# A list-scheduled attention and mixture kernel on one core: the planner's weights and its assumed DMA landing time replaced

## The chip, the core and the metric

One core of a Trainium2 chip runs the whole program. The metric is device microseconds of one execution; several executions of a kernel are timed and their median is given. TensorE is called PE here (its weight loads PEld), VectorE DVE, ScalarE ACT, GpSimd POOL, and SP is the engine whose queue issues all the DMAs. L12 is line 12 of the kernel. The changed kernel has one line more in its table and two more in `build`, so a line of the changed kernel stands 3 higher than the same line before; the text uses the numbers of the kernel before.

## What is computed

```python
# attention: batch 4, heads 8, sequence 576, head size 64, causal, with a bias from a cumulative sum
cum = np.cumsum(np.maximum(s, 0.0), axis=-1)
bias = -(cum[:, :, :, None] - cum[:, :, None, :])
scores = np.where(causal, -1000000000.0, scale * q @ k.T + np.minimum(bias, 0.0))
x = softmax(scores) @ v                      # 2304 tokens x 512
# first layer
h = x @ w_in                                 # 512 x 1024
solu = h * softmax(h)
x = (layernorm(solu) * g_ln) @ w_out         # 1024 x 512
# second layer
h = maximum(maximum(x @ w1, x @ w2), x @ w3) # 512 x 768 each
out = h @ w_out2                             # 768 x 512
```

## The kernel before

All inputs are float32. The kernel computes every matrix product from float16 halves: a value is split into a high half and a low half (the rest), and three products (high high, high low, low high) are added in PSUM. Much of the work outside PE is this splitting. Weights come in as float32 words and are unpacked once (`load_w`): L608, L612 and L615 on DVE sort the bits of a piece of 512 columns into a PSUM accumulator, L620 on ACT writes the high half, L622 on DVE the low half. There are 40 such pieces.

The 2304 tokens are 18 tiles of 128: four blocks of 128 rows for each of two sequences (`c` = 0, 1), then one tail tile with the last 64 rows of both, and the same again for the other two sequences. Score widths are 128, 256, 384 and 512 columns for the blocks and 576 for the tail. For each tile `prep` loads k, q and v and splits them (`st`, `vs`), `scores` makes the score matmuls of a pair of heads (L788, L794), a maximum on DVE (L825, L858) and the exponential on ACT (L877, into `r`), and splits the probabilities into `es`; the last 64 columns of a tail tile go into `est`. A DMA transposes `es` into `et` and `est` into `ett` (L904, L911). `values` multiplies by v (L961, for tails L942 and L948) and normalises into `f` (L995). `m1` is the first layer's first product (L1034) with its softmax and layer norm (L1048 to L1096) into `ln` and, transposed, `lnt`. Each two tiles make a group, for which follow `m2` (L1131), the three products of `m3` with their running maximum (L1170, L1189), and `m4` (L1204), whose rows go out. The first four tiles are transposed on PE instead (L474, L488), with ACT or DVE copying the halves out of PSUM (L481, L484, L491, L492).

`split_ops` makes the two steps of a split. Each can stand on several engines: the high half (L405 on ACT, L407 on DVE or POOL), the low half on DVE as one instruction (L434) or on POOL as two, a scaling in place (L441) and a subtraction (L444). L1095 (DVE or POOL) or L1096 (ACT) scales `e`.

The order of all this is not written by hand. `Schedule.run` replays the program in a model: each operation has a duration for each engine it may stand on, a position `pos` (its urgency, a tile number shifted by the weights in the table `P`: `la`, `wi`, `w3`, `o2` and so on) and its dependences and buffers. The engine that can begin something first takes the operation with the smallest `pos` among those that could begin then. Where an operation may stand on several engines, `spare` is added to the end on each (DVE, ACT, POOL; first three numbers up to position `spare_until`, the next three after), and the smallest sum decides. A DMA is taken to land `LAT_DMA` (ns) after its share of the queue's traffic. The model holds POOL and those DVE operations that are not in `ALONE` apart: one runs at a time. The order that the replay gives is what is emitted, engine by engine; on the chip each engine runs its list in order.

```python
    LAT_SAME, LAT_CROSS, LAT_DMA, LAT_ISSUE = 130, 180, 1250, 650
...
                    end = t + o.alts[c[1]][1] + sp[e] - 1
...
                o.end = dma + self.LAT_DMA
```

Of the kernel before, what the change touches and what calls it, by code (L numbers as in the profile page):

```python
# [30 lines left out]
MINUS_ONES = -(1.0 + 0xBF80 * 2.0 ** -23)  # L31

P = dict(
    la=8.4,
    lp=-1.469,
    lu=-13.333,
    lv=-0.647,
    o1=-3.616,
    o2=-4.09,
    o3=-0.398,  # L40
    o4=0.334,
    ds=1.887,
    wi=-20.819,
    wid=2.708,
    wo=-15.551,
    wod=-18.167,
    w3=6.958,
    w3d=1.141,
    w4=-16.623,
    w4d=15.675,  # L50
    mp=-1.93,
    look=[2.7, 0.0, 35.7, 169.7, 69.9],
    spare=[1764.9, 1665.2, 1871.5, 968.8, -1500.0, 3960.7, 27.5],
    n_st=4,
    gs=[2, 2, 2, 2, 2, 2, 2, 2, 2],
    wa=["ldq0", "ldq0", "c00", "c00"],
    nf=3,
    net=4,
    nr=3,
    lc=-23.89,  # L60
    S=[],
    ep=[0],
    pt=[4, 4, 4, 4],
# [288 lines left out]
def build(nc, T, X, dims):  # L352
# [15 lines left out]
    size = [len(ts) * 128 for ts in groups]  # L368
    due = [ts[-1] for ts in groups]
    S_ = Schedule(P["look"], P["spare"], P["off"], P["eng"])  # L370

    def unit(name, tile=""):
        S_.unit, S_.tile = name, tile

    op = S_.op
    pools = {}
# [126 lines left out]
    def scaled(k):  # L503
        return k in P["S"] or f"{k}@{S_.tile}" in P["S"]

# [646 lines left out]
    def m3(g, f0):  # L1152
# [11 lines left out]
        for w in range(3):  # L1164
            ps, first = buf("acc"), ([], [])
            for f in (f0, f0 + 1):
                for kk in range(KD):
# [8 lines left out]
                    o.after.update(before)  # L1176
                    S_.hold(o, m)
                    o.after.update(first[f % 2])
# [68 lines left out]
    for k, n in enumerate(P["wa"]):  # L1247
        if n in named:
            for i in range(2):
                if ("w", k, i) in named:  # L1250
                    named["w", k, i].after.add(named[n])
    return S_, pools


@with_exitstack
def fox_attention_solu_max3_kernel(
# [71 lines left out]

    X = dict(q=q, k=k, v=v, s=s, w_in=w_in, w_out=w_out, g_ln=g_ln, w1=w1, w2=w2, w3=w3, w_out2=w_out2, out=out)
    sched, pools = build(nc, T, X, (B, H, S, D, DFF, DF2))  # L1330
    sched.run()
    with tc.manual_schedule():
# [34 lines left out]
```

## Time and profile before

| | us |
|---|---|
| median of 3 runs | 676.64 (675.38 to 676.77) |
| the profiled execution | 676.31, span 674.6 |
| PE busy | 621.2 (92%) |
| DVE busy | 464.3 (69%) |
| ACT busy | 301.8 (45%) |
| POOL busy | 34.1 (5%) |

An engine's busy time is the union of its instructions; PE's weight loads run beside its matmuls. Windows are in us from the start of the span. In the rows below, "[1.29 <-DMA ett<-est]" is the time that the engine was idle before the row, and what ended it.

### The profile page before, as it was taken

Reading aid. Unit: us, or ns where it says so; the run is one execution under the profiler, and the core shown is the slowest. Engines: PE = TensorE matmul, PEld = TensorE weight load, DVE = VectorE, ACT = ScalarE, POOL = GpSimd, SP = SyncE. Lnnn points to the kernel's source line nnn. Section 1 sums busy time; section 2 is a strip of 40 time slices with the busy share of each in tenths; the row PEclk is TensorE's granted clock in tenths of the full one; section 3 lists DMA queues with packets and bytes.
Section 4 is the critical chain, followed back from the end, with each engine's and each line's share of the span. In section 5 each row is a group of like instructions: output and inputs, shape, how many; then the busy total and the mean of one; then the engine's idle time right before and its main releaser. Section 6 shows DMA issues by size and latency. Waiting matters only on the chain.

```text
span 674.6 us, 15275 instructions
## 1 busy us (share of the span) xinstructions
PE 621.2 (92%) x6188; PEld 442.7 (66%) x6188; DVE 464.3 (69%) x1109; ACT 301.8 (45%) x713; POOL 34.1 (5%) x49
## 2 busy tenths in 40 slices
PE   1579888899999999899999999989999999999997
PEld 1334556777576666667666675659767867878774
DVE  7899999997799678798888988775155245212121
ACT  3678875554476445667556546351023022110110
POOL 1101000010001101020000201000000000000000
PEclk9998999999999999999999999989999999999999
DMA  6976755569989879699999896864032022000001
GB/s 176 276 216 176 171 153 162 172 144 186 170 167 176 155 142 150 131 186 189 162 181 174 152 181 119 127 99 84 1 63 63 1 48 48 1 32 2 17 17 32
DMA packets 249351, 82.68 MB, mean 123 GB/s; under 512 B 225472, under 2 KB 244096, under 8 KB 249280
## 3 DMA queue, kind: packets, MB, share of 16 engines
q1 hardware_dynamic: 249280, 81.70, 60.0%
q8 instruction: 48, 0.79, 0.5%
q14 instruction: 23, 0.19, 0.1%
HBM read 35.95 MB, written 4.83 MB: 60 GB/s over the span
## 4 chain that ended last, share of the span: by engine, by line
PE 63%; DVE 15%; DMA 14%; issue 3%; ACT 3%; SPq 1%; POOL 0%; DVEq 0%; POOLq 0%; ACTq 0%
PE acc L1170 23%; PE acc L1131 11%; PE acc L1204 9%; PE h L1034 8%; DMA et<-es 7%; PE sc L794 4%; PE av L961 3%; PE sc L788 2%; DVE acc L612 2%; DVE acc L615 2%; DVE r L825 1%; DMA kt<-in_moe_w_in_dram 1%; DMA vs<-in_moe_w_in_dram 1%; DVE f L608 1%; DMA lnt<-ln 1%
## 5 line engine op out<-in xcount | busy, mean ns | idle before, releaser
L1170 PE MATMUL acc<-x2A,w_h 128*128 128x256 f16 x1296 | 215.5, 273 | 2.3 <-DVE f L1189 1.5
L1170 PEld LDWEIGHTS <-w_h 128*128 128x128 f16 x1944 | 187.3, 98 | 32.6 <-issue 7.6
L1170 PE MATMUL acc<-x2B,w_h 128*128 128x256 f16 x648 | 176.7, 273 | 0.0
L877 ACT ACTIVATE r<-r,mn 128x128 f32<-128x128 f32 (+4 forms) x144 | 83.0, 578 | 55.0 <-DVE mn L825 39.7
L1034 PE MATMUL h<-w_in_h,xt 128*128 128x512 f16 x432 | 101.3, 380 | 0.0
L1131 PE MATMUL acc<-lnt,w_out_h 128*128 128x256 f16 x864 | 98.2, 273 | 1.1 <-DMA lnt<-ln 1.0
L1131 PEld LDWEIGHTS <-w_out_h 128*128 128x128 f16 x864 | 83.4, 98 | 13.3 <-issue 3.3
L1189 DVE TENSOR_TENSOR f<-f,acc 128x512 f32<-128x512 f32 x54 | 36.9, 684 | 69.8 <-PE acc L1170 69.8
L1034 PEld LDWEIGHTS <-xt 128*128 128x128 f16 x432 | 40.0, 98 | 45.7 <-issue 3.6
L454 ACT ACTIVATE f<-acc 128x512 f32<-128x512 f32 x37 | 22.0, 595 | 98.5 <-PE acc L1170 57.9
L1204 PE MATMUL acc<-w2o_h,h2A 128*128 128x512 f16 x216 | 64.4, 380 | 0.0
L825 DVE CUSTOM_DVE_ANT_0 r<-sc,mask 128x128 f32<-128x128 f32 (+3 forms) x128 | 58.7, 485 | 7.1 <-PE sc L794 5.5
L434 DVE SCALAR_TENSOR_TENSOR es<-r,es 128x512 f16<-128x512 f32 (+1 forms) x89 | 56.7, 642 | 2.3 <-ACT es L405 1.7
L794 PE MATMUL sc<-kt,qt 64*128 64x256 f16 (+2 forms) x768 | 47.9, 264 | 0.7 <-DMA kt<-st 0.4
L961 PE MATMUL av<-vs,et 128*128 128x64 f16 x960 | 38.1, 195 | 5.1 <-DMA et<-es 4.8
L961 PEld LDWEIGHTS <-et 128*128 128x128 f16 x960 | 34.9, 99 | 12.0 <-DMA et<-es 7.7
L405 ACT ACTIVATE es<-r 128x512 f16<-128x512 f32 (+1 forms) x48 | 28.0, 584 | 29.4 <-DMA et<-es 25.5
L1204 PE MATMUL acc<-w2o_h,h2B 128*128 128x512 f16 x108 | 41.0, 379 | 0.0
L1055 ACT ACTIVATE ln<-e,st 128x1024 f32<-128x1024 f32 x18 | 20.7, 1150 | 42.4 <-DVE e L1048 35.7
L788 PE MATMUL sc<-ckr,cqr 6*128 6x128 bf16 (+5 forms) x192 | 28.6, 308 | 11.9 <-DMA cqr<-cum_d 9.8
L794 PEld LDWEIGHTS <-qt 64*128 64x128 f16 (+1 forms) x864 | 26.8, 99 | 18.3 <-issue 11.2
L454 ACT ACTIVATE x2A<-acc 128x512 f16<-128x512 f32 x16 | 9.5, 593 | 64.0 <-PE acc L1131 64.0
(138 smaller groups left out, 721.3 us busy)
## 6 DMA issues: line engine op xcount, KB each, us to landing
kt<-in_moe_w_dram SPq DMA_DIRECT2D x18, 256.0 KB
vs<-in_moe_w_dram SPq DMA_DIRECT2D x18, 256.0 KB
raw<-in_k_dram SPq DMA_DIRECT2D x16, 256.0 KB
raw<-in_q_dram SPq DMA_DIRECT2D x16, 256.0 KB
raw<-in_v_dram SPq DMA_DIRECT2D x16, 256.0 KB
out_dram<-f SPq DMA_DIRECT2D x16, 256.0 KB
kt<-in_moe_w_out_dram SPq DMA_DIRECT2D x7, 512.0 KB
vs<-in_moe_w_out_dram SPq DMA_DIRECT2D x7, 512.0 KB
```

The costliest lines, as they stand in the source:

```text
L434: nc.vector.scalar_tensor_tensor(out=lo(g), in0=src(g), scalar=sc1(g), in1=hi(g), op0=ALU.mult, op1=ALU.subtract)
L454: nc.scalar.activation(out=out(*a), in_=in_(*a), func=AF.Copy, scale=scale)
L788: yield lambda: nc.tensor.matmul(out=out(), lhsT=T["cqr"][cr, hp, cs], rhs=T["ckr"][cr, hp, ck], start=True, stop=False, skip_group_check= ...
L794: yield lambda n=n, qa=qa, o=o, kx=kx: nc.tensor.matmul(out=out()[:, o], lhsT=qv()[r, qa * HP + hp, ts], rhs=kx, start=False, stop=(n == 2 ...
L825: nc.vector.tensor_tensor_reduce(out=gw(R)[:, g], in0=gw(sc[y])[:, g], in1=T["mask"][:, SM - W:SM], scale=1.0 / S_MUL, scalar=3e38, op0=AL ...
L877: nc.scalar.activation(out=gw()[:, g], in_=gw()[:, g], func=AF.Exp, bias=mnf()[:, g:g + 1], scale=-1.0, accum_out=den(hs[g]),)
L961: nc.tensor.matmul(out=out, lhsT=ea_[:, ea, kb], rhs=T["v_s"][c, kb // 2][:, kb % 2, ha + a, va], start=(kb == 0 and m == 0), stop=(kb == ...
L1034: nc.tensor.matmul(out=hb()[:, n * 512:(n + 1) * 512], lhsT=xt()[:, xa, kk], rhs=T["w_in_h"][:, wa, kk, n * 512:(n + 1) * 512], start=(kk ...
L1131: nc.tensor.matmul(out=ps()[:, d % 2 * GN:(d % 2 + 1) * GN], lhsT=T["w_out_h"][:, wa, kk, d * 128:(d + 1) * 128], rhs=lnt()[:, la, kk], st ...
L1170: nc.tensor.matmul(out=ps()[:, f % 2 * GN:(f % 2 + 1) * GN], lhsT=T["w123_h"][:, w, wa, f, kk], rhs=x2(xa)[:, kk], start=(kk == 0 and i == ...
L1189: op([("DVE", dve2(2 * GN), lambda ps=ps: nc.vector.tensor_tensor(out=m(), in0=m(), in1=ps(), op=ALU.max))], pk + [m], [m], pos, kind="m3x")
L1204: nc.tensor.matmul(out=ps(), lhsT=h2(ha)[:, f, o * 128:(o + 1) * 128], rhs=T["w2o_h"][:, wa, f], start=(f == 0 and i == 0), stop=(f == KF2 ...
```

## The change

The numbers of the table `P` are replaced, and the model's landing time becomes a number of the table, 1.7 us where 1.25 stood. No instruction's shape and no arithmetic is changed; order and choice of engine come out of the same replay.

```diff
 P = dict(
-    la=8.4,
+    la=7.686,
...
-    w3=6.958,
-    w3d=1.141,
+    w3=11.379,
+    w3d=2.467,
...
-    look=[2.7, 0.0, 35.7, 169.7, 69.9],
-    spare=[1764.9, 1665.2, 1871.5, 968.8, -1500.0, 3960.7, 27.5],
+    look=[0.0, 0.0, 35.7, 25.4, 16.3],
+    spare=[1756.4, 1670.1, 1222.0, 2565.6, -1500.0, 5079.4, 23.5],
...
-    lc=-23.89,
+    lat=1.7,
+    lc=-29.521,
...
     S_ = Schedule(P["look"], P["spare"], P["off"], P["eng"])
 
+    S_.LAT_DMA = int(P["lat"] * 1000)
+
```

What the new order holds, by count over the whole program: the instructions of PE are the same in number and kind. Of the high halves (L405, L407), 104 stood on ACT, 91 on DVE and 16 on POOL; now 70 stand on ACT, none on DVE and 141 on POOL. Of the low halves, 12 stood on POOL (L444), now 48, and DVE's L434 fall from 199 to 163. L1095 falls from 10 to 0 on DVE and rises from 0 to 12 on POOL.

The first place is POOL's list where the first L1204 matmul comes (`vs`, `st` and `es` are halves of v, of k and q, and of the probabilities; `raw` is what was loaded). Before:

```order
L407 TENSOR_SCALAR st_87<-raw_85 128x512
L407 TENSOR_SCALAR h2A_112<-f_114 128x512
L441 TENSOR_SCALAR raw_85<-raw_85 128x512
L444 TENSOR_TENSOR st_86<-raw_85,st_86 128x512
L441 TENSOR_SCALAR r_90<-r_90 128x384
```

The last row stands behind the first L1204 matmul. After the change:

```order
L410 TENSOR_SCALAR st_87<-raw_84 128x512
L444 TENSOR_SCALAR raw_84<-raw_84 128x512
L447 TENSOR_TENSOR st_87<-raw_84,st_87 128x512
L1098 TENSOR_SCALAR e_106<-e_106,st_123 128x1024
...
L1098 TENSOR_SCALAR e_106<-e_106,st_124 128x1024
L410 TENSOR_SCALAR h2A_112<-f_116 128x512
L410 TENSOR_SCALAR st_86<-raw_84 128x512
L410 TENSOR_SCALAR vs_73<-raw_85 128x8x64
...
L410 TENSOR_SCALAR es_93<-r_90 128x384
L410 TENSOR_SCALAR es_93<-r_92 128x384
L410 TENSOR_SCALAR es_94<-r_90 128x384
```

Three more rows of `es`, with two of `vs` and `st` among others, follow ahead of the first L1204 matmul. POOL now makes halves of k, q, v and of the probabilities, and scales `e`: up to there it had ten such instructions and now has 33.

The second place is PE near the end of the attention, between the last score matmuls of the last head pair of the last tile and the value matmuls of the head pair ahead of it, which read `ett` and `et`. Before:

```order
L794 MATMUL sc_126<-k_tail,qt_89 64x64
L1204 LDWEIGHTS h2A_112
L1204 MATMUL acc_131<-w2o_h,h2A_112 128x512
...
L1170 LDWEIGHTS w_h
L1170 MATMUL acc_129<-x2A_110,w_h 128x256
...
L942 LDWEIGHTS ett_101
L942 MATMUL av_127<-v_tail,ett_101 128x64
```

Between them stand 12 matmuls of 512 columns (L1204) and 6 of 256 (L1170). After the change:

```order
L797 MATMUL sc_126<-k_tail,qt_89 64x64
L1207 LDWEIGHTS h2A_112
L1207 MATMUL acc_131<-w2o_h,h2A_112 128x512
...
L1207 MATMUL acc_129<-w2o_h,h2A_112 128x512
...
L945 LDWEIGHTS ett_101
L945 MATMUL av_127<-v_tail,ett_101 128x64
```

Now 15 matmuls of 512 columns stand there. Over the whole way from the scores of that head pair to its value matmuls, it is 21 of 512 and 6 of 256 before, and 30 of 512 after.

The third place is PE behind its first score matmuls (`r` are the first probabilities, `acc` the three accumulators that weights are unpacked in as well). Before:

```order
L794 MATMUL sc_126<-kt_68,qt_88 128x128
L474 MATMUL acc_131<-k_tail,r_90 128x128 x4
L474 MATMUL acc_129<-k_tail,r_91 128x128 x4
L488 LDWEIGHTS k_tail
L488 MATMUL acc_131<-et_97,k_tail 128x512
```

After the change:

```order
L797 MATMUL sc_126<-kt_68,qt_88 128x128
L477 MATMUL acc_130<-k_tail,r_90 128x128 x4
L477 MATMUL acc_131<-k_tail,raw_85 128x128 x4
L491 LDWEIGHTS k_tail
L491 MATMUL acc_130<-et_97,k_tail 128x512
```

The first probabilities are transposed into another accumulator, and a tile of k comes ahead of the second ones.

## Rows read from the trace of the kernel before

**Rows 1.** The page, first part: busy time, share of the span, instructions.

```profile
PE 621.2 (92%) x6188; PEld 442.7 (66%) x6188; DVE 464.3 (69%) x1109; ACT 301.8 (45%) x713; POOL 34.1 (5%) x49
```

**Rows 2.** Three stretches: length, each engine's busy time (instructions), granted clock, DMA share, GB/s.

```profile
0.00:131.60 131.60, 95.70 (x768) 61.87 (x769) 122.19 (x289) 85.44 (x201) 9.03 (x19) 0.99 0.69 189
131.60:450.00 318.40, 305.55 (x3573) 211.37 (x3573) 266.25 (x679) 178.49 (x433) 24.81 (x29) 1.00 0.90 158
450.00:674.60 224.60, 219.98 (x1852) 169.46 (x1849) 75.84 (x143) 37.84 (x80) 0.24 (x1) 0.99 0.14 33
```

**Rows 3.** PE's waits: what ended them, us in total, times, longest.

```profile
PE sc L788 <- DMA cqr<-cum_d: 9.8, 2, 8.8
...
PE av L961 <- DMA et<-es: 4.8, 9, 1.0
PE av L942 <- DMA ett<-est: 3.3, 2, 2.0
...
PE acc L1131 <- DMA lnt<-ln: 1.0, 1, 1.0
```

**Rows 4.** PE in order of time, four rows behind idle time: start, us.

```profile
17.04 0.55 PE L788 MATMUL sc<-ckr,cqr 6*128 6x128 bf16 x2 [8.85 <-DMA cqr<-cum_d]
...
25.69 1.94 PE L474 MATMUL acc<-k_tail,r 128*128 128x128 f32 x8 [5.71 <-DVE w_in_h L622]
...
270.86 0.23 PE L942 MATMUL av<-v_tail,ett 128*128 128x64 f16 x2 [1.29 <-DMA ett<-est]
...
448.51 0.29 PE L942 MATMUL av<-v_tail,ett 128*128 128x64 f16 x2 [2.00 <-DMA ett<-est]
```

**Rows 5.** The chain that ended last, one transpose: start, us, what.

```profile
444.91 3.56 DMA ett<-est
```

**Rows 6.** DVE, groups by line and shape: count, busy us, mean ns, idle before.

```profile
L434 DVE SCALAR_TENSOR_TENSOR es<-r,es 128x512 f16<-128x512 f32 x58 | 39.8, 689 | 1.5 <-ACT es L405 1.1
...
L434 DVE SCALAR_TENSOR_TENSOR es<-r,es 128x384 f16<-128x384 f32 x31 | 16.8, 554 | 0.8 <-ACT es L405 0.6
...
L407 DVE TENSOR_SCALAR es<-r 128x512 f16<-128x512 f32 x29 | 12.8, 441 | 13.5 <-DMA et<-es 12.5 <-ACT r L877 1.0
...
L1095 DVE TENSOR_SCALAR e<-e,st 128x1024 f32<-128x1024 f32 x10 | 8.1, 807 | 0.0
...
L407 DVE TENSOR_SCALAR es<-r 128x384 f16<-128x384 f32 x12 | 4.3, 356 | 8.9 <-DMA et<-es 8.9
...
L434 DVE SCALAR_TENSOR_TENSOR est<-r,est 128x64 f16<-128x64 f32 x15 | 3.1, 216 | 0.1
```

**Rows 7.** POOL, groups by line and shape.

```profile
L444 POOL TENSOR_TENSOR st<-raw,st 128x512 f16<-128x512 f32 x3 | 3.8, 1261 | 0.2
...
L407 POOL TENSOR_SCALAR st<-raw 128x512 f16<-128x512 f32 x3 | 1.9, 617 | 44.4 <-DMA raw<-in_q_dram 26.1 <-DMA raw<-in_k_dram 18.3
...
L407 POOL TENSOR_SCALAR ln<-e 128x1024 f16<-128x1024 f32 x1 | 1.2, 1222 | 0.4 <-ACT e L1096 0.4
...
L441 POOL TENSOR_SCALAR r<-r 128x64 f32<-128x64 f32 x1 | 0.7, 738 | 19.7 <-ACT est L405 19.7
...
L444 POOL TENSOR_TENSOR est<-r,est 128x64 f16<-128x64 f32 x1 | 0.3, 304 | 0.1
```

**Rows 8.** POOL and DVE in order of time, from 221 us.

```profile
221.19 2.14 POOL L444 TENSOR_TENSOR ln<-e,ln 128x1024 f16<-128x1024 f32 x1 [11.86 <-ACT ln L405]
...
222.53 1.36 DVE L434 SCALAR_TENSOR_TENSOR xs<-f,xs 128x512 f16<-128x512 f32 x1
```

**Rows 9.** The chain that ended last, two dense pieces of PE.

```profile
474.17 10.48 PE acc L1131 x96
484.65 5.18 PE h L1034 x24
```

**Rows 10.** The stretch behind the gap at 448 us, columns as in rows 2.

```profile
448.20:451.60 3.40, 3.09 (x56) 3.01 (x56) 3.23 (x8) 1.21 (x3) 0.00 (x0) 0.50 0.96 184
```

**Rows 11.** ACT in order of time, the last exponential of the first probabilities.

```profile
22.87 0.39 ACT L877 ACTIVATE r<-r,mn 128x128 f32<-128x128 f32 x1
```

More of the change, by code (lines that the diff above doesn't have):

```diff
@@ L33 @@
 P = dict(
-    la=8.4,
[L35 to L46, printed above, removed]
-    w3=6.958,
-    w3d=1.141,
-    w4=-16.623,
-    w4d=15.675,
-    mp=-1.93,
-    look=[2.7, 0.0, 35.7, 169.7, 69.9],
-    spare=[1764.9, 1665.2, 1871.5, 968.8, -1500.0, 3960.7, 27.5],
+    la=7.686,
+    lp=-1.305,
+    lu=-12.094,
+    lv=-1.314,
+    o1=-3.698,
+    o2=-7.479,
+    o3=-0.356,
+    o4=0.384,
+    ds=1.084,
+    wi=-20.747,
+    wid=2.836,
+    wo=-18.656,
+    wod=-15.917,
+    w3=11.379,
+    w3d=2.467,
+    w4=-14.324,
+    w4d=10.963,
+    mp=-1.525,
+    look=[0.0, 0.0, 35.7, 25.4, 16.3],
+    spare=[1756.4, 1670.1, 1222.0, 2565.6, -1500.0, 5079.4, 23.5],
     n_st=4,
```

## The prediction

> **What bounds the kernel now.** I read the page's engine totals first, then a table of three stretches, then PE's waits. PE is busy 621.2 of 674.6 us; the reader should see that no other engine comes near it over the whole [rows 1]. By stretch the picture splits [rows 2]. In the first 131.6 us PE works only 95.7 us while DVE works 122.2 (93%): DVE sets the pace there, because it unpacks the weights. From 131.6 to 450 us PE is busy 305.5 of 318.4 and DVE 266.3. After 450 us there is only dense work, PE 220 of 224.6. The change neither adds nor removes a matmul, so what it can win is PE's idle time and what it can lose is new idle time.
>
> PE's waits [rows 3] name the causes. The 9.8 us for cqr is almost wholly one gap of 8.85 us at 17 us; 5.7 us is one gap at 25.7 us, on a decode step that holds an accumulator [rows 4]. What is left for DMAs after 131.6 us is et 4.8, ett 3.3, lnt 1.0 and cqr 9.8 - 8.85 = 0.95, together 10.05 us. These are hand-overs in which transposed probabilities landed after PE came to their value matmuls; the two longest are the tail tiles' ett, 1.29 and 2.00 us [rows 4]. A transpose takes some 3.6 us from the end of its issue to its landing [rows 5].
>
> **Step 1: up to the first L1204 matmul, where DVE is full.** I count, in the order in which the planner emits all engines, everything that stands ahead of the first L1204 matmul. DVE loses three L407 of 384 columns (3 x 0.356), four of 512 (4 x 0.441), two L434 of the k and q tiles (2 x 0.689, the row of es), one L1095 (0.807) and, net, one eviction of 512 columns (0.69, priced as L434): 5.7 us. It gains three L434 es and one L825 of 384 columns (4 x 0.554) and one L1148 (0.69): 2.9 us. Net -2.8 us [rows 6]; two short instructions on 8 columns are left out. ACT loses some evictions too; nothing waits long for it here, so I count that at zero.
>
> The same stretch has 23 more POOL instructions: nine L407 of 512 columns (9 x 0.617), two L441 (2 x 0.617), two L444 (2 x 1.261), four of 1024 columns now at L1095 (4 x 1.222, by the nearest row, L407 ln) and six es halves (at most 0.617 each): 17.9 us [rows 7]. POOL itself has room: it is busy 34 us of 675. But its work is not free for DVE. The L434 that writes xs takes 1.36 us when it falls into POOL's 2.14 us L444, against 0.69 for the same shape on es [rows 6, 8]. After 20 us, POOL has 37 instructions with 30.8 us of work; 16 DVE instructions that overlap one (the first at 24.0 us, the last at 454.9) are longer than the median of their form, by 6.4 us in all, and none of them reads PSUM. So DVE lost 6.4 / 30.8 = 0.21 us for each us of POOL. At that share the 17.9 us cost 3.8 us, and step 1 comes to -2.8 + 3.8 = +1.0 us. The bounds are -2.8 (POOL finds only gaps) and 17.9 - 2.8 = +15.1 (DVE stands still for all of it). I take the measured share.
>
> **Step 2: 131.6 to 450 us, the hand-overs.** Counting matmuls in the new order between the last score matmul of a head pair and its first value matmul, with 0.109 us for 256 columns, 0.216 for 512 [rows 9] and a quarter of the first for 64, gives PE's lead over the chain of maximum, exponential, split and transpose. For the 32 head pairs of the 384 and 512 wide tiles the median lead rises from 14.8 to 17.4 us, and 26 of them get longer. For the eight tail pairs it rises from 10.3 to 11.3. At the 2.00 us gap (the third head pair of the last tile) the lead has 21 matmuls of 512 columns and 6 of 256 before and 30 of 512 after: 5.19 to 6.48 us, +1.3, the scores and values between being the same. At the 1.29 us gap it has 21 of 512 and 39 of 256 before, 12 and 75 after: +2.0 us.
>
> The chain gets longer as well. The high halves of es move to POOL (68 of 92, against 3 before): 0.617 us there against 0.441 on DVE, so at most 0.2 us more [rows 6, 7]. The low halves of est all move: L441 0.738 plus L444 0.304 on POOL where one L434 of 0.216 stood on DVE, +0.8 us [rows 6, 7]. So the two ett gaps shrink by 1.3 - 0.8 = 0.5 and 2.0 - 0.8 = 1.2, together 1.7. The et waits, nine of 0.5 us on a mean, are covered by 2.6 us more lead except for the two pairs of one tile where it falls (20.8 to 14.8 and 18.7 to 14.3); I leave 0.8 us of them, so -4.0. Lnt and cqr I leave as they are. Step 2 gives -5.7 us; its bounds are 0 and -10.05.
>
> **Step 3: the clock.** In 448.2 to 451.6, right behind the 2.00 us gap, the granted clock is 0.50, which is 1.2 GHz, over 3.4 us, so up to 1.7 us is lost there [rows 10]. That gap only shrinks and others may come, so I take 0, with 1.7 either way.
>
> **Step 4: the tail.** The halves of h2 move to POOL at the end too. An L407 on POOL is 0.617 us against 0.441 on DVE, 0.18 more [rows 6, 7], and the final L1204 reads the late halves only after 12 matmuls of 512 columns, 2.6 us. The last maximum (priced as L434), the high half and the low half take 0.69 + 0.62 + 0.69 = 2.0 us: hidden, with 0.6 us to spare. If that went, it would cost some tenths once.
>
> **Sum.** +1.0 - 5.7 + 0 = -4.7 us. The profiled execution took 676.3 us (span 674.6), 0.3 under the median of 676.6; 676.3 - 4.7 = 671.6, on the scale of the medians **671.9 us**.
>
> **Rivals.** *More is won.* POOL finds the gaps in DVE's day (step 1 at -2.8), and the 5.7 us gap shrinks: the new order puts the first probabilities into the accumulator that is free, so their transposition could begin when the last of their exponentials ends, 23.3 us, rather than at 25.7, so -2.4 us [rows 4, 11]. With step 2 that is -10.9: 665.7 us. Against it: the decode work that was ahead still has to be done, and DVE is the one that is full.
>
> *The waits move.* The transposes land as planned, but the slower halves come late to DVE's lows and DVE, in order, holds the scans behind them. If this gives back what step 2 wins beyond 1 us, the time stays at 676.6. For it: for each of the 68 es halves that POOL now writes, an L434 on DVE waits. Against it: DVE has 52 us of idle time in the middle stretch [rows 2].
>
> *Slower: DVE held by POOL.* In that stretch each us of POOL costs s us of DVE and so of PE. The time is 676.6 - 2.8 - 5.7 + 17.9 s. It passes 676.6 by 0.2% (1.35 us, about the least that the measurement tells from no change) at s = 0.55. At 0.7 it is 680.6. For it: DVE is 93% busy there, so POOL seldom finds it idle, while the 0.21 is a mean over the whole run. Against it: the scans and evictions, which read PSUM, are not lengthened. The Trainium skill, "SBUF — State Buffer", section "Who interferes with whom", calls the port pair that the two engines share an exclusive lock, so that the second to issue blocks until the first ends; if that struck every new POOL instruction at full length, s would be 1 and the time 686.0. The lengthened L434 agrees with the lock; the 0.21 says that it seldom strikes at full length.
>
> That the change does nothing is excluded by the two orders: 91 L407 stand on DVE before and none after.
>
> **Chances.** Forecast 0.45, more won 0.15, waits move 0.15, held by POOL 0.25. The first two of these are faster by over 0.2%: 0.60; same 0.15; slower 0.25. The range runs from the larger gain to the POOL case at 0.7: **665 to 681 us**; the likeliest case alone spans 668 to 675 (half of step 2, s up to 0.4).
>
> **What would show it.** Right: POOL near 160 us busy; DVE some 30 to 40 us less; PE's waits for et and ett after 131.6 us under half of 8.1 us; PE idle in the first 131.6 us as before (36 us) within 3 us; L434 means up by tens of ns. Wrong: PE's idle time early up by 5 us or more with lengthened L612 or L434 rows beside POOL (the slower rival), or the et waits unchanged while waits on POOL appear (the waits moved).

## The result, and the profile after

| | us |
|---|---|
| before, median of 4 runs | 676.70 (675.38 to 677.26) |
| after the change, median of 4 runs | **665.51** (663.38 to 666.45) |
| ratio | 0.9833, interval 0.9802 to 0.9863 |
| the profiled execution after | 663.38, span 661.7 |

Faster, as forecast, by 11.2 us (1.7%, interval 1.4 to 2.0) where 4.7 were forecast. The time lies 0.5 us above the lower end of the range, next to the rival "More is won" (665.7). From here on, rows of the changed kernel carry its own line numbers (3 higher than before; in kernels with a helper function, 9 to 34 higher than before).

The page's first part after:

```profile
PE 620.3 (94%) x6188; PEld 443.0 (67%) x6188; DVE 419.2 (63%) x968; ACT 285.2 (43%) x681; POOL 179.9 (27%) x245
```

Against [rows 1], PE's work is the same, DVE has lost 45 us, ACT 17, and POOL has gained 146. The three stretches, columns as in [rows 2]:

```profile
0.00:131.60 131.60, 99.25 (x751) 62.42 (x752) 122.97 (x286) 81.88 (x198) 20.61 (x32) 0.97 0.70 192
131.60:450.00 318.40, 314.43 (x3575) 223.54 (x3573) 231.35 (x560) 162.57 (x400) 130.50 (x171) 1.00 0.87 154
450.00:661.70 211.70, 206.61 (x1871) 157.04 (x1867) 64.87 (x124) 40.77 (x85) 28.82 (x43) 1.00 0.18 40
```

The idle time of PE (length less busy) falls from 35.9 to 32.4 us in the first stretch and from 12.9 to 4.0 in the second; in the third it is 5.1 for 4.6. Most of what idle time shows is in the middle. PE's waits after, what ended them, us in total, times, longest:

```profile
PE sc L791 <- DMA cqr<-cum_d: 9.2, 2, 6.5
PE acc L477 <- DMA raw<-in_k_dram: 5.7, 2, 4.8
PE av L964 <- DMA et<-es: 3.1, 4, 1.2
PE acc L477 <- POOL e L1098: 2.4, 1, 2.4
PE acc L477 <- ACT r L880: 1.7, 1, 1.7
PE acc L477 <- DVE w_in_h L625: 1.5, 1, 1.5
...
PE av L945 <- DMA ett<-est: 0.9, 2, 0.5
PE sc L791 <- DVE mn L828: 0.3, 1, 0.3
```

Beside [rows 3]: et falls from 4.8 to 3.1, ett from 3.3 to 0.9, lnt is gone, and of cqr all that is left is the start. Two more rows of before go with this list, the wait for the scores' bank (`mn`), which falls to 0.3, and one for a tile of k, which stays:

```profile
PE acc L474 <- DMA raw<-in_k_dram: 4.9, 1, 4.9
...
PE sc L788 <- DVE mn L825: 1.7, 4, 0.9
```

The gap of 5.71 us at 25.7 us in [rows 4] has become two shorter ones, and at 87 us there is a new wait, on a scaling of `e` that now stands on POOL. PE in order of time:

```profile
22.01 1.63 PE L477 MATMUL acc<-k_tail,r 128*128 128x128 f32 x4 [1.69 <-ACT r L880]
25.09 1.12 PE L477 MATMUL acc<-k_tail,raw 128*128 128x128 f32 x4 [1.46 <-DVE w_in_h L625]
...
87.42 0.72 PE L477 MATMUL acc<-k_tail,e 128*128 128x128 f32 x4 [2.44 <-POOL e L1098]
```

For all kernels below I add up the idle times above 0.06 us ahead of PE's instructions: "front" is up to PE's 800th matmul (135 to 148 us, depending on the kernel), "middle" from there to the 4336th (450 us before, 451 after). In that account before has 35.8 and 12.7, after 32.3 and 4.0, and later 0.0 and 0.5: 48.5 and 36.7 together, 11.8 of the 12.9 us between the two profiled spans. The middle's 8.7 us are et and ett 8.5 to 3.6 (-4.9), mn 1.8 to 0.3 (-1.5), and lnt, cqr and kt 2.4 to nothing.

Idle time is not the whole account, since PE can also be busy for longer. The kernels have two places at which exactly the same matmuls are done, by count of every kind: ahead of PE's 801st matmul and ahead of its 5013th. PE at these two places, before:

```profile
135.56 0.27 PE L1170 MATMUL acc<-x2B,w_h 128*128 128x256 f16 x1
...
520.96 0.38 PE L1170 MATMUL acc<-x2A,w_h 128*128 128x256 f16 x2
```

After the change:

```profile
137.13 0.27 PE L1173 MATMUL acc<-x2B,w_h 128*128 128x256 f16 x1
...
508.06 0.38 PE L1173 MATMUL acc<-x2A,w_h 128*128 128x256 f16 x2
```

So the changed kernel is 1.6 us behind at the first place and 12.9 ahead at the second, and behind that both take 153.6 us. All of the gain, 14.5 us, falls between the two, although the idle time of that way falls by 8.3 only (12.7 to 4.4); and the first part comes out later, although its idle time falls by 3.5.

### The profile page after: what moved, and what is told of

Read it like the earlier page. It is cut to its first block, busy times and chain, and to the rows that moved or that the text cites. A ratio compares the mean times of both kernels' runs of the same rounds, so it can differ in the third digit from the quotient of the medians.

```text
span 661.7 us, 15427 instructions
## 1 busy us (share of the span) xinstructions
PE 620.3 (94%) x6188; PEld 443.0 (67%) x6188; DVE 419.2 (63%) x968; ACT 285.2 (43%) x681; POOL 179.9 (27%) x245
## 4 chain that ended last, share of the span: by engine, by line
PE 74%; DVE 10%; DMA 8%; ACT 2%; SPq 2%; issue 2%; POOL 1%; DVEq 0%; POOLq 0%
PE acc L1173 27%; PE acc L1134 13%; PE acc L1207 11%; PE h L1037 9%; PE sc L797 5%; PE av L964 4%; DMA et<-es 3%; PE sc L791 2%; DVE acc L615 2%; DMA kt<-in_moe_w_in_dram 2%; DVE acc L618 2%; DMA raw<-in_k_dram 1%; PE av L951 1%; DMA ett<-est 1%; DVE r L828 1%
## 5 line engine op out<-in xcount | busy, mean ns | idle before, releaser
L1134 PEld LDWEIGHTS <-w_out_h 128*128 128x128 f16 x864 | 84.8, 99 | 12.7 <-issue 1.8
L410 POOL TENSOR_SCALAR es<-r 128x512 f16<-128x512 f32 (+1 forms) x68 | 48.2, 709 | 99.8 <-DMA et<-es 50.2
L437 DVE SCALAR_TENSOR_TENSOR es<-r,es 128x512 f16<-128x512 f32 (+1 forms) x86 | 60.5, 710 | 19.5 <-POOL es L410 16.0
L828 DVE CUSTOM_DVE_ANT_0 r<-sc,mask 128x128 f32<-128x128 f32 (+3 forms) x128 | 58.6, 487 | 17.1 <-PE sc L797 15.5
L410 POOL TENSOR_SCALAR h2A<-f 128x512 f16<-128x512 f32 x19 | 11.7, 617 | 121.3 <-DVE f L1192 116.8
L1098 POOL TENSOR_SCALAR e<-e,st 128x1024 f32<-128x1024 f32 x12 | 15.4, 1282 | 97.8 <-DVE st L1093 87.3
L964 PE MATMUL av<-vs,et 128*128 128x64 f16 x960 | 36.7, 194 | 3.5 <-DMA et<-es 3.1
L1151 DVE SCALAR_TENSOR_TENSOR x2B<-acc,x2A 128x512 f16<-128x512 f32 x18 | 12.4, 691 | 39.6 <-ACT x2A L457 39.5
```

Of the source, the lines that this page charges most:

```text
L410: eng.tensor_scalar(out=out(g), in0=src(g), scalar1=sc(g), scalar2=1.0, op0=ALU.mult, op1=ALU.mult)
L437: nc.vector.scalar_tensor_tensor(out=lo(g), in0=src(g), scalar=sc1(g), in1=hi(g), op0=ALU.mult, op1=ALU.subtract)
L828: nc.vector.tensor_tensor_reduce(out=gw(R)[:, g], in0=gw(sc[y])[:, g], in1=T["mask"][:, SM - W:SM], scale=1.0 / S_MUL, scalar=3e38, op0=AL ...
L964: nc.tensor.matmul(out=out, lhsT=ea_[:, ea, kb], rhs=T["v_s"][c, kb // 2][:, kb % 2, ha + a, va], start=(kb == 0 and m == 0), stop=(kb == ...
L1134: nc.tensor.matmul(out=ps()[:, d % 2 * GN:(d % 2 + 1) * GN], lhsT=T["w_out_h"][:, wa, kk, d * 128:(d + 1) * 128], rhs=lnt()[:, la, kk], st ...
```

## The experiments

Three theories were set against each other: **leads** (longer ways on PE between scores and values end the waits for the transposes), **POOL** (a relieved DVE gives the gain), and **scramble** (any newly worked out order differs by some us, and this one is a good one). The first and the last are not exclusive; the runs weigh them. The ratio is to the kernel before, run beside each on the same chip, where its medians were 676.7 to 678.1. "Low" is the time between 46 and 650 us in which the granted clock was 0.50. "801st" is where PE's 801st matmul starts, "on to 5013th" the time from there to the start of the 5013th; the rest took 153.6 us in every kernel.

| kernel | median us | ratio, interval | front | middle | et+ett after front | mn after front | low | 801st | on to 5013th |
|---|---|---|---|---|---|---|---|---|---|
| before | 676.7 | 1 | 35.8 | 12.7 | 8.5 | 1.8 | 6.8 | 135.6 | 385.4 |
| b_pool | 678.2 | 1.0017, 0.9987 to 1.0046 | 36.4 | 14.6 | 8.2 | 2.6 | 13.7 | 138.9 | 386.2 |
| b_lat17 | 677.1 | 1.0006, 0.9979 to 1.0032 | 38.7 | 8.5 | 4.5 | 3.3 | 10.2 | 141.1 | 378.7 |
| b_lat1200 | 683.3 | 1.0080, 1.0052 to 1.0109 | 40.0 | 13.8 | 10.0 | 3.6 | 10.2 | 141.3 | 387.3 |
| b_lat1300 | 678.7 | 1.0013, 0.9985 to 1.0040 | 37.5 | 10.2 | 4.5 | 2.9 | 20.5 | 139.4 | 384.5 |
| b_more10 | 686.5 | 1.0140, 1.0069 to 1.0210 | 35.7 | 17.9 | 6.2 | 8.2 | 20.5 | 136.5 | 396.0 |
| b_ahead | 677.3 | 0.9991, 0.9965 to 1.0017 | 33.8 | 14.0 | 10.3 | 2.4 | 13.6 | 136.2 | 388.3 |
| **after** | 665.5 | 0.9833, 0.9802 to 0.9863 | 32.3 | 4.0 | 4.1 | 0.3 | 6.8 | 137.1 | 370.9 |
| a_dve | 669.9 | 0.9904, 0.9866 to 0.9941 | 33.0 | 3.9 | 4.2 | 0.3 | 6.8 | 138.0 | 373.7 |
| a_lat125 | 673.2 | 0.9944, 0.9916 to 0.9972 | 34.5 | 11.9 | 6.2 | 0.6 | 20.5 | 135.2 | 385.9 |
| a_lat165 | 674.2 | 0.9951, 0.9929 to 0.9973 | 32.8 | 11.4 | 5.4 | 4.4 | 13.7 | 136.9 | 383.9 |
| a_lat175 | 675.0 | 0.9965, 0.9950 to 0.9979 | 37.7 | 4.8 | 2.1 | 2.2 | 20.5 | 147.9 | 374.2 |
| a_lat18 | 670.6 | 0.9900, 0.9865 to 0.9936 | 32.8 | 8.0 | 1.6 | 4.0 | 10.2 | 137.1 | 378.4 |
| a_less2 | 676.9 | 0.9978, 0.9955 to 1.0002 | 32.8 | 11.1 | 10.1 | 1.9 | 6.8 | 137.9 | 381.9 |
| a_less5 | 702.4 | 1.0366, 1.0333 to 1.0400 | 33.4 | 28.4 | 29.9 | 1.6 | 20.5 | 136.8 | 411.6 |
| a_more5 | 666.4 | 0.9827, 0.9789 to 0.9865 | 32.9 | 4.8 | 1.0 | 2.8 | 3.4 | 137.1 | 373.1 |
| a_sel | **663.2** | 0.9785, 0.9752 to 0.9819 | 33.3 | 2.5 | 1.2 | 1.1 | 3.4 | 137.4 | 370.3 |

The account columns come from one profiled execution each, which can stand 2 or 3 us off the median (a_lat125's was its slowest, 676.4).

### The casts alone, in either order

**b_pool** and **a_dve** keep PE's order word for word and change the engine of the casts only, where the operations are emitted:

```diff
         for o in sched.order:
+            if len(o.alts) == 3 and o.eng == "DVE":
+                o.fn = [f for e, _, f in o.alts if e == "POOL"][0]
             o.fn()
```

(a_dve has the same with the two engines' names exchanged.)

> The order before, instruction for instruction on PE, with one thing changed: each cast of the high halves (es, and the second of L1095) that has three engines to choose from and stood on DVE is put on POOL in its place (about 101 instructions). Three theories. Leads (the change won by putting more PE work between scores and values, so that the DMAs et and ett land in time): the leads here are those of before, so 676 us, +-2, and the waits on et and ett keep their 8.1 us; if POOL's slower cast comes on the chain, up to 680. POOL (the change won because DVE was relieved): about 668, with PE's idle time of 12.9 us between 131.6 and 450 us down to 4 to 8. Scramble (any other order differs from before by some us either way, the change was a good draw): no forecast, the time anywhere between 672 and 682.

> The order of the change, instruction for instruction on PE, with each cast that has three engines to choose from put back from POOL on DVE in its place (153 instructions), so that DVE has as much as before and a little more. Leads: the leads stay, so the middle stretch keeps its gain; what is lost is DVE's in the first 131.6 us, at most 3 us: 666 to 669. POOL: the gain is gone, 674 to 678. Scramble: 665 to 680.

Casts on POOL in the order before win nothing: 1.0017, no difference that can be told. A DVE with less to do was not what that order lacked; its et and ett waits stay (8.2 us). Casts on DVE in the new order give back 4.4 of the 11.2 us by the medians; the front's 33.0 and the middle's 3.9 us of idle time hardly differ from the change's (1.3 us more stand behind the middle). The order alone, with the casts as before, thus keeps most of it: 11.7 of the 14.5 us between the two places, 385.4 to 373.7. So the order of the work carries most of the gain, and POOL's share has a value only within it. a_dve lay a little above what leads foretold and far below POOL's 674; POOL alone as the cause has fallen.

### The longer landing alone, and the weights alone

```diff
-    LAT_SAME, LAT_CROSS, LAT_DMA, LAT_ISSUE = 130, 180, 1250, 650
+    LAT_SAME, LAT_CROSS, LAT_DMA, LAT_ISSUE = 130, 180, 1700, 650
```

That is **b_lat17**. **a_lat125** is the change with `lat=1.25`.

> The order worked out with the longer landing alone (1.7 us in place of the one before), the weights of urgency as before: the casts of the high halves stay on DVE, the leads in the steps of the second and third head group grow to a median of 17.0 us and the smallest of the tail to 11.4. Leads: the waits on et and ett after 131.6 us fall from 8.1 to under 3 us and the time to 670, +-2. POOL: 676, since DVE is as loaded as before. Scramble: 670 to 682, with waits elsewhere than before.

> The weights of urgency of the change, with the shorter landing of before: the casts go to POOL as in the change (145 of them), the leads fall to a median of 15.9 us and in the tail to 12.4 (before: 14.8 and 10.3; the change: 17.4 and 11.3). Leads: between the two kernels, 668 to 672, with 2 to 5 us of waits on et and ett. POOL: as the change, 665.5, +-1.5. Scramble: 664 to 678.

b_lat17's waits did much of what leads said (et and ett 4.5 for 8.5 us, under 3 foretold), but the time did not follow: behind the 801st matmul 6.7 us are won, and ahead of it 5.5 are lost. a_lat125 comes out 1 us above the leads' 668 to 672 and inside scramble's range, which was 14 us wide. Neither half of the change gives its share of the whole. That asked for more draws.

### Five neighbours

Each of these changes only the assumed landing, by 0.05 or 0.1 us, and so has the replay work the order out anew: `lat` 1.65, 1.75 and 1.8 with the change's weights, `LAT_DMA` 1200 and 1300 with those of before. a_lat18 was run first.

> The weights of urgency of the change with a landing of 1.8 us assumed in place of 1.7: a new order with longer leads (median 18.3 us, tail 14.9) and the same share of casts on POOL. Leads or POOL: the time of the change or less, 663 to 666. Scramble: 668 or more, with the waits moved to other places, the first 140 us above all, where the order is redrawn.

> The weights of the change with 1.65 us of landing assumed for 1.7: the order is worked out anew, with leads a little shorter (median 16.8 us, tail 11.1) and the same casts on POOL. Rules (longer leads and casts on POOL give the gain, whatever the order): 665 to 668. Scramble (every order worked out is a draw that differs from the next by some us in places that no rule speaks of, and the change kept a good one): 668 to 676, as the two draws at 1.25 and 1.8 us (673.2 and 670.6).

> The same with 1.75 us (median 16.3 us, tail 13.9). Rules: 664 to 667. Scramble: 668 to 676.

> The weights of before with 1.20 us of landing for 1.25: the order drawn anew, with leads (median 15.1 us, tail 9.8) and engines of the casts all but as before. Rules: 677, +-2. Scramble: 679 or more, if the weights of before too were kept because their order was a good draw; and then the change's weights are better by the difference of the two families' middles, not by 11 us.

> The same with 1.30 us (median 14.8 us, tail 12.4). Rules: 675 to 677. Scramble: 679 or more.

All three neighbours of the change are slower than it by 5 to 9.5 us, although the one at 1.8 us has longer median leads. The rules alone have fallen here; the scramble's numbers held in all three. For the weights of before 683.3 fits its 679 or more, and 678.7 can't be told from before (ratio 1.0013). The mean ratio of the four redraws with the change's weights (1.25, 1.65, 1.75, 1.8) is 0.9940, that of the three with those of before (1.20, 1.30, 1.70) is 1.0033. The difference, 0.93% or 6.3 us, is what the change's weights are worth from one draw to the next, an estimate from seven draws; the remaining 5 us of 11.3 are that the change's own order is further ahead of its neighbours than the order before is of its own.

Part of what a neighbour loses is single stalls and the clock behind them, and where they fall differs: a_lat175 loses 10.8 us to the change ahead of the 801st matmul, a_lat165 13.0 behind it. a_lat165 has one on PE at 228 us, in order of time:

```profile
228.03 0.37 PE L791 MATMUL sc<-ckr,cqr 6*128 6x512 bf16 x1 [2.63 <-DVE mn L828]
```

and in a table by stretch, behind it, a granted clock of 0.50 (the third number from the end), which is 1.2 GHz:

```profile
229.60:236.40 6.80, 5.29 (x43) 2.70 (x43) 3.17 (x8) 2.44 (x6) 1.24 (x2) 0.50 1.12 183
236.40:241.00 4.60, 4.23 (x56) 3.77 (x55) 2.33 (x6) 0.81 (x2) 2.04 (x3) 1.00 0.86 164
```

a_lat18 has the like at 230.8 us (2.35 us), a_lat125 at 140.1 (3.04 us), and a_lat175 three of 1.5 to 2.3 us between 85 and 104 us on weight pieces, with 17 us at 0.50 among them. The order of the change has one such place, at 87.4 us:

```profile
87.90:94.70 6.80, 6.12 (x27) 3.85 (x26) 6.77 (x14) 4.70 (x11) 0.00 (x0) 0.50 0.52 153
```

### The leads within one order

To move leads without a new draw, **a_less2** and **a_less5** take the change's finished order and put each value product ahead of up to 2 or 5 dense steps that stood before it, where no dependence or buffer forbids it; **a_more5** and, in the order before, **b_more10** put it behind up to 5 or 10 that followed. The helper's core:

```diff
+def sooner(order, n, first):
+    dense = ("m1", "m2", "m3", "m4")
...
+    for o in [o for o in order if o.kind == "av"]:
+        if int(o.unit[1:].split(".")[0]) < first:
+            continue
+        for _ in range(n):
+            i = order.index(o)
+            p = next((j for j in range(i - 1, -1, -1) if order[j].eng == "PE"), None)
+            if p is None or order[p].kind not in dense:
+                break
...
+    sooner(sched.order, 5, 4)
     with tc.manual_schedule():
```

> The order of the change with one thing undone: each value product of the steps with 384 and 512 wide tiles and of the tail is put ahead of up to five dense PE steps that stood before it, so that its lead falls to what it was before or a little under (median 15.7 us and 10.1 in the tail; before 14.8 and 10.3; the change 17.4 and 11.3). Engines of the casts, and the first 60 us, as in the change. Leads: the waits on et and ett come back, from 4.0 to 8 us or more, and the time is 668 to 672. POOL: 665.5, +-1. Scramble (each order worked out is a draw, and the change kept a good one): no change beyond the waits on et and ett that a trace shows.

> The order of the change with each value product put ahead of up to two dense PE steps that stood before it (lead in the steps of 384 and 512 wide tiles 16.8 us for 17.4, tail 10.6 for 11.3). Knee (the change's leads end just where the chain of scores, casts and transposing DMA ends, and every us less is waited for at each of some 30 products): 675 to 685, with 12 to 18 us of waits on et and ett. Slope by the forecast's price (2.6 us of lead were worth 5.7 us): 667 to 668.

> The order before with the value products put behind the dense PE steps that followed them (median lead 15.9 us for 14.8, smallest 9.8 for 8.8; tail 11.1 for 10.3), all else as before. Leads: the waits on et and ett fall from 8.1 to 3 or 4 us, the time by as much, to 673. POOL: 677, as before. Scramble: as Leads, since the order is kept.

> The change with the same shift once more: value products behind up to five dense steps that followed them (median lead 18.7 us, tail 12.7). Leads: of the 4.0 us of waits on et and ett that are left, 1 or 2 stay, so 663, unless et and ett, held longer, now make the casts wait: then 666 or more.

Taking a median of 1.7 us of lead away costs 36.9 us, and 0.6 us costs 11.3, by the medians. PE's waits of a_less5:

```profile
PE av L995 <- DMA et<-es: 23.9, 28, 2.2
...
PE av L976 <- DMA ett<-est: 5.3, 3, 1.9
```

28 waits for et where the change has 4, and five new stretches of 3.4 us at 0.50, four of them right behind such a wait of 1.5 us or more. In the change's order, then, the products stand just behind the landings: a knee, as a_less2's 676.9 says (the way on to the 5013th matmul is 11 us longer than in the change, the way to the 801st 0.8); its waits (10.1 us) came out a little less than the 12 foretold. One limit: the helper shortened leads in the small tiles of the second half below those of before as well, so a_less5 is no image of the old leads.

Past the knee nothing is won by moving all (a_more5: et and ett 1.0 us for 4.1, mn 2.8 for 0.3, time the same), and in the order before it loses 9.4 us. PE's waits of b_more10, and below them DVE's:

```profile
PE sc L819 <- DVE mn L856: 7.8, 10, 1.5
...
PE av L992 <- DMA et<-es: 3.2, 6, 1.0
```

```profile
DVE f L1026 <- PE av L992: 11.3, 7, 3.6
DVE f L1020 <- PE av L979: 8.2, 2, 4.8
```

Before, these two waits of DVE were shorter:

```profile
DVE f L989 <- PE av L948: 5.0, 2, 3.5
...
DVE f L995 <- PE av L961: 0.7, 2, 0.5
```

DVE reads the products' sum into `f` at its old place in its own list; when the product comes later, DVE stands there, and the pass over the next scores, queued behind, frees its PSUM bank late: PE waits for mn. So a longer lead can cost something at the reader of the product, which a replay moves too and a shift on one engine does not.

**a_sel** moves only the six products that still waited by 0.3 us or more in the change, by the helper that puts products later, with a list of their places:

```diff
+    later(sched.order, 4, (21, 23, 28, 34, 52, 69))
```

> The change with only the six value products that waited for a DMA by 0.3 us or more after 131.6 us put behind up to four dense steps that followed them. If the waits on et and ett are lost time: 2 to 4 us of them go, 662 to 663.5. If every shift on PE is paid back by DVE, which reads the product's sum in its own fixed order and then keeps the next scores' bank: 665.5, with waits on mn in their place.

PE's waits of a_sel, beside those of the change above:

```profile
PE sc L822 <- DVE mn L859: 1.0, 2, 0.7
...
PE av L976 <- DMA ett<-est: 0.7, 1, 0.7
...
PE av L995 <- DMA et<-es: 0.4, 2, 0.2
```

et and ett fall from 4.0 to 1.1 us, 0.7 comes back as mn. The time is 663.17 (662.94 to 664.08, 5 runs), 2.3 us under the change's median; the ratios are 0.9785 (0.9752 to 0.9819) and 0.9833 (0.9802 to 0.9863). The intervals overlap, and the two were not run side by side: probably the fastest of the kernels here, not shown to be.

### The gap at 25 us

**b_ahead** takes the order before and moves one DVE instruction, the low half of the fourth weight piece, ahead of the first pass over scores:

```diff
+def ahead(order, k):
...
+    o = [o for o in order if o.kind == "wl"][k]
+    i, p = order.index(o), next(j for j, x in enumerate(order) if x.kind == "ttr")
...
+    order.insert(p, order.pop(i))
...
+    ahead(sched.order, 3)
```

> The order before with one DVE instruction moved: the low half of the fourth piece of w_in (ready at 20.4 us by the profile, run at 24.87) goes ahead of the first pass over scores at 21.38, so that its PSUM buffer is free for the transposition of r. If that buffer is what PE waits for at 25.69: the gap of 5.71 us falls by about 2.3 (to the last exp of the first four heads, 23.35), and PE is ahead by 0.8 to 2 us at its 100th matmul and the time 675 to 676. If not: the same gap under another name, 677.

PE of b_ahead, in order of time:

```profile
22.62 1.64 PE L483 MATMUL acc<-k_tail,r 128*128 128x128 f32 x4 [2.78 <-ACT r L886]
26.73 1.08 PE L483 MATMUL acc<-k_tail,r 128*128 128x128 f32 x4 [2.48 <-DVE w_in_h L631]
27.61 0.63 PE L497 MATMUL acc<-et,k_tail 128*128 128x512 f16 x1
```

The buffer was what PE waited for: the gap falls from 5.71 to 2.78 and now ends with the exponentials. But four transpositions later PE waits 2.48 us for the next piece's low half, its 100th matmul starts at 36.0 us as before, and the time is 677.3, no difference. The same gap under another name.

## Why the prediction was right or wrong

The direction was right, the size was not: 4.7 us forecast, 11.2 measured. The two profiled executions are 12.9 us apart: +1.6 us up to the 801st matmul, -14.5 from there to the 5013th, nothing behind it. Against these stand +1.0, -5.7 and 0. Each is read from one execution of a kernel, but kindred kernels agree: the 801st matmul starts at 135.6 to 136.5 us in before, b_more10 and b_ahead and at 136.8 to 137.9 in the change and its four shifted orders, and the way on to the 5013th takes 385.4 to 388.3 in before, b_pool and b_ahead and 370.3 to 373.1 in the change, a_more5 and a_sel. So the term of the sum that failed is step 2, which is short by 8.8 us; what steps 1 and 3 had wrong nearly cancels.

**Step 1 (first part, +1.0)** has about the size of the +1.6 measured, by luck. It was the sum of -2.8 us for DVE and +3.8 for POOL's hold on DVE, at 0.21 us per us of POOL. Neither shows: in the same order, the casts on POOL bring the 801st matmul 0.9 us sooner than the casts on DVE (137.1, a_dve 138.0), and in the order before 3.3 us later (b_pool), one execution each. PE's idle time in the first 131.6 us fell by 3.5 us, and it falls with the order, not with the casts: 33.0 us with all casts back on DVE (a_dve), 36.4 with them on POOL in the old order (b_pool), by the account of idle times. By exclusion it is set by the order of weight pieces, accumulators and first tiles, which the step did not weigh, and no single gap of it is worth its own length (b_ahead). What takes the 3.5 us back is the clock, under step 3. The share itself was mis-sized too. Adding up how far DVE instructions that overlap one of POOL exceed the shorter ones of their form, after 20 us, gives 15.5 us for 177 us of POOL, 0.09, and 0.16 in the front, where before had 6.5 for 30.8. POOL bears a part. Groups by line and shape, of DVE and then of POOL:

```profile
L437 DVE SCALAR_TENSOR_TENSOR es<-r,es 128x512 f16<-128x512 f32 x57 | 43.8, 775 | 15.2 <-POOL es L410 13.5 <-ACT es L408 1.6
```

```profile
L410 POOL TENSOR_SCALAR es<-r 128x512 f16<-128x512 f32 x46 | 34.0, 740 | 71.9 <-DMA et<-es 39.9 <-ACT r L880 17.5 <-DVE st L1078 6.7
...
L410 POOL TENSOR_SCALAR h2A<-f 128x512 f16<-128x512 f32 x19 | 11.7, 617 | 121.3 <-DVE f L1192 116.8 <-DVE den L979 4.4
```

DVE's low half takes 775 ns where it took 689 [rows 6], and POOL's cast 740 where the same instruction on h2 takes 617 and one before took 617 [rows 7]. DVE also waits 13.5 us for POOL's high halves for `es` of 512 columns alone ("the waits move" had this mechanism), which costs PE nothing visible in a stretch where DVE has 87 us to spare.

**Step 2 (-5.7) failed by its size**; its mechanism was right. Its own term, et and ett, came to -4.9 us of idle time against -5.7. What it missed is two things. It left mn, lnt, cqr and kt as they were, which gave another 3.9; together -8.7, which as idle time is inside the bounds of 0 to -10.05; the time is not. And it took a wait to be worth the idle time that the profile prints, where the way from the 801st to the 5013th matmul is 14.5 us shorter with 8.3 us less idle time and 8 waits in place of 22. Of the other 6.2, some 2.4 are an estimate of what the waits hide: printed idle time begins where the matmul before is drawn to end, and a value product of 64 columns is drawn 194 ns long while the next one starts 29 ns after it when nothing is waited for. Some 1.2 are the stretch at 0.50 behind the 2.00 us gap [rows 10], which is gone. The rest, 2.6, was not traced; a_less2, with as much idle time there as before (12.7), is still 3.5 us shorter. A price of a lead per us (as the forecast for a_less2 takes it) does not hold either: 0.6 us of lead is worth 11 us there, a knee. The step counted the nine products that did wait, and not how many stand just behind their landing. That the chain gets longer was right in sign (POOL's cast 740 ns for DVE's 441); that the new order needs its longer leads for it is not shown, as a_dve has the same waits (4.2 us).

**Step 3 (0, with 1.7 either way) failed too.** The first rise of the clock comes 12 us later (last section), and behind the new wait at 87.4 us there is a stretch of 6.8 us at 0.50 where before had 3.4 us at 52 us. PE busy up to the first rise and in that stretch, before:

```profile
0.00:31.70 31.70, 11.64 (x81) 7.22 (x81) 26.00 (x61) 14.14 (x34) 6.02 (x15) 1.00 0.77 219
52.20:55.60 3.40, 3.37 (x19) 2.19 (x19) 3.40 (x10) 1.50 (x3) 0.00 (x0) 0.50 0.66 166
```

After the change, up to its first rise (the 1.00 of either rise row is printed without a record, see the last section):

```profile
0.00:43.50 43.50, 23.11 (x135) 12.16 (x136) 37.76 (x96) 21.90 (x57) 6.40 (x16) 1.00 0.81 224
```

With the 6.12 us above, PE is busy 29.2 us at the lower level where it was 15.0. At 631 against 379 ns for the same matmul (last section) these 14.2 us cost some 5.7 more, an estimate; with 3.5 us less idle time that makes +2.2 in the front, +1.6 measured. [Rows 2] print 0.99 for this part, so the forecast could not see it there. In the whole, PE's time from first to last matmul less its idle times hides this (616.6 us before, 615.5 after), in part because the busy time that waits hid behind the front is gone.

**Step 4 (0)** held: 153.6 us from the 5013th matmul to the end in both, with no idle time from the last halves.

**The rivals.** "More is won" had the number, not the way: it asked for DVE's 2.8 and for 2.4 us at the 25 us gap. Of PE's idle time up to its 50th matmul, 19.7 us before and 17.4 after, 2.3 us did go in the new order, but the 100th starts at 35.8 us for 35.9 before; b_ahead shows that ending this gap by itself wins nothing, and a_dve that DVE's relief was not the rest. "Held by POOL" asked for a longer first part and a time above 676; the first part is 1.6 us longer, but a_dve, without these casts on POOL, is no sooner. "The waits move" is excluded by the time. What no case held was that one order out of many with the same rules can be 5 us better than its neighbours. Of the signs named, POOL's busy time (180 for 160), DVE's (45 less for 30 to 40), the L434 means (689 to 775 ns) and the et and ett waits (4.0 us, just under half of 8.1) came, the first two by more than was said; "PE idle in the front as before within 3 us" missed by half a microsecond, and idle time alone was the wrong sign to watch.

**Open.** How the change's order was found can't be seen in a run; that it is the best draw of five with its weights is what the runs show. How much of POOL's 4.4 us in the new order is the load and how much the plan's fit to its own engines was not separated.

## What to carry to other kernels

Where a planner sets the order, a difference between two tables of numbers is two things: what the rules are worth, and which draw each table got. Run neighbours (a hair's change of one number) before crediting a rule: here they spread over 1%. A lead ahead of a DMA had a knee here, not a slope: give waiting products what they need one by one (a_sel), and look at the reader when you move the product. A gap's length is not its price: look for what stands right behind it. And idle time is not the time: compare where the same work is done, which here showed a first part that waits less and ends later.

## What the runs showed of the hardware

The clock that the profile prints before a run's first clock record is not a measurement. After the change, PE by line and shape between 24 and 43 us, and then between 44 and 60:

```profile
L1037 PE MATMUL h<-w_in_h,xt 128*128 128x512 f16 x7 | 3.2, 631 | 0.0
```

```profile
L1037 PE MATMUL h<-w_in_h,xt 128*128 128x512 f16 x24 | 6.2, 379 | 0.0
```

A table by stretch prints a granted clock of 1.00 for 32 to 43.5 us as for 43.5 to 55, but the same matmul takes 631 and 379 ns. Before, L474 of 128 columns takes 424 ns between 20 and 31 us and 280 to 287 between 32 and 43, where L1034 takes 379. In a_dve, whose order on PE is the same and whose record begins earlier, the granted clock is told:

```profile
12.00:42.60 30.60, 19.77 (x125) 10.52 (x126) 28.26 (x81) 16.91 (x50) 1.78 (x2) 0.50 0.90 255
42.60:55.00 12.40, 11.03 (x95) 6.37 (x93) 11.76 (x29) 9.91 (x22) 0.00 (x0) 1.00 0.83 245
```

So the change runs at 1.2 GHz until 43.5 us, with PE 9.8 us busy of the 11.5 ahead of the rise, where before rose at 31.7; a_lat125, with the change's weights, rose at 29.9. Of PE's 9.8 us there, 631 against 379 ns says that up to 3.9 could be saved, an estimate. No run here tried it by itself.
